# Softmax weights normalized ahead of their transposes instead of on the output

## The chip, the cores and the metric

The kernel runs on one core of a Trainium2 chip. Its time is the device time in microseconds of one execution, and lower is better. The engines of the core are TensorE (PE; its weight loads are listed as PEld), VectorE (DVE), ScalarE (ACT), GpSimd (POOL) and SyncE (SP), which here issues the DMAs. Each engine works through its own instructions in order; where an instruction waits, everything behind it on that engine waits too.

## The reference, cut to what matters

An attention over 8 batches, 12 heads, 448 positions and 64 elements per head feeds a gated feed-forward block.

```python
q_n, k_n = rmsnorm(q, g_q), rmsnorm(k, g_k)
scores = scale * np.matmul(q_n, k_n.transpose(0, 1, 3, 2))
scores = scores - np.max(scores, axis=-1, keepdims=True)
attn = np.exp(scores)
attn = attn / (np.sum(attn, axis=-1, keepdims=True) + 1e-09)
attn_out = np.matmul(attn, v)
...
h = gelu(x @ w_in)                       # x: attention output, heads side by side
u, v = h[..., :d_ff // 2], h[..., d_ff // 2:]
v_n = layernorm(v) * g_ln
v_s = np.einsum('ts,bsd->btd', w_sg, v_n) + b_sg[None, :, None]
out = x + (u * v_s) @ w_out
```

The division of the weights by their row sums is what the change moves. Since the sum belongs to a row of `attn`, the division can be made on the weights or, row by row, on the product with `v`.

## The kernel before, in words

Values are kept to more than 16 bits by splitting each into a high and a low f16 part and adding three products (high x high, high x low, low x high).

Heads are taken in pairs (48 pairs, `i`), and two pairs make a unit (24 units, `u`). The 448 rows of the two pairs of a unit are laid end to end, 896 rows, and cut into seven tiles of 128 rows (`t` = 0 to 6). Tile 3 holds the last 64 rows of the first pair and the first 64 of the second.

`scores(u)` (L375) goes through the seven tiles. For each, PE makes the scores of both heads, 128 rows by 2 x 448 (L389: 6 matmuls, 12 for tile 3), in a PSUM tile `s`, of which there are two (`NS`). DVE takes the negated maximum of each row and head (L392). ACT replaces the scores by their exponentials, one instruction per head, which also adds up the row (L394, with a short ACTIVATION_READ_ACCUMULATOR that writes the sum). After a `yield`, ACT copies the exponentials of both heads as f16 into `ahl` (L397), DVE subtracts that copy from the exponentials for the low part (L398), and SP issues the DMA transpose of the tile into `at_all` (L403). When L398 has ended, the PSUM tile is free for the next but one score tile.

`pv(i)` (L431) multiplies the transposed weights with `v` (L446, 24 matmuls) in the one buffer of the PSUM pool `ps_v` (`NV` = 1). The output has the 128 elements of the two heads on the partitions and the 448 positions along the free dimension. A row sum is therefore needed as a row along the free dimension, the same on all 64 partitions of a head. `recips(i)` (L406) makes it at the start of `pv`: POOL adds 1e-9 to the sums (L413), DVE takes reciprocals (L414), POOL splits them (L415, L416), PE multiplies each column, broadcast, with an identity matrix (L423, 16 matmuls per pair), and ACT copies the result to SBUF as `row` (L426). That product also uses the buffer of `ps_v`. At the end of `pv` DVE multiplies the output by `row` (L450), ACT copies it as f16 (L453) and DVE makes the low part (L454).

Around this run the preparation of q and k (`squares`, `norms`, `split`: L308 to L338), that of v (`vsquares`, `vscale`, `vsplit`: L343 to L371), the decoding of the weights at the start (`weights`) and, for each batch, the feed-forward block `moe` (L477).

The order of the work: all these are generators. The loop over pairs takes steps of `scores`, `pv`, `weights` and `moe` in turn, in the proportions of `SC`, `SV`, `WR` and `M0` to `ML`. The order in the program gives priorities, `moe` gets later ones by `MOFF`, and a planner (`schedule_with_timeline_sim`) then fixes each engine's order from its own estimate of durations. Semaphores are set from the data dependences. So a different set of instructions also gives a somewhat different order of the others.

Of the kernel before, what the change touches and what calls it, by code (L numbers as in the profile page):

```python
# [8 lines left out]
F32 = mybir.dt.float32  # L9
F32R = mybir.dt.float32r  # L10
F16 = mybir.dt.float16
BF16 = mybir.dt.bfloat16
I32 = mybir.dt.int32
AF = mybir.ActivationFunctionType
ALU = mybir.AluOpType
# [5 lines left out]
LEAST_SQ = (1.125 * 2.0 ** -15) ** 2  # L21
ASC = 2.0 ** 14


MOFF, MOFF0, GP = 200, 100, 350

# [5 lines left out]

VC, UC = (3,), (0, 1)

SC, SV = 7, 4

NS, NV, NM = 2, 1, 3
NQK, NVR, RAWB = 2, 2, 3
# [8 lines left out]
def kernel(  # L47
# [15 lines left out]
    B, H, S, D = q.shape  # L63
    P = 128
# [7 lines left out]
    HP = P // 2  # L72
    CM = S // P
    SM = CM * P
    CK = CM + 1
    C7 = 2 * CM + 1
    C4 = CM + 1
    NG = 2
# [4 lines left out]
    const = ctx.enter_context(tc.tile_pool(name="const", bufs=1))  # L83
    ld = ctx.enter_context(tc.tile_pool(name="ld", bufs=3))
    prep = ctx.enter_context(tc.tile_pool(name="prep", bufs=2))
    att = ctx.enter_context(tc.tile_pool(name="att", bufs=2))
    sml = ctx.enter_context(tc.tile_pool(name="sml", bufs=4))
    xp = ctx.enter_context(tc.tile_pool(name="xp", bufs=NX))
    ps_s = ctx.enter_context(tc.tile_pool(name="ps_s", bufs=NS, space=bass.MemoryType.PSUM))
    ps_v = ctx.enter_context(tc.tile_pool(name="ps_v", bufs=NV, space=bass.MemoryType.PSUM))  # L90
# [3 lines left out]
    V, A, G = nc.vector, nc.scalar, nc.gpsimd  # L94
    mm = nc.tensor.matmul
# [3 lines left out]
    G.memset(ones, 1.0)  # L99
    ident = const.tile([P, P], BF16, name="ident")  # L100
    make_identity(nc, ident)
    ident_h = const.tile([P, P], F16, name="ident_h")
    A.activation(out=ident_h, in_=ident, func=AF.Copy)
    swap = const.tile([P, P], F32, name="swap")
    for d, e in ((0, HP), (HP, 0)):
        V.tensor_copy(out=swap[:, d:d + HP], in_=ident[:, e:e + HP])
# [159 lines left out]
    R, U = {}, {}  # L266
    lo, hi = slice(0, HP), slice(HP, P)
# [107 lines left out]
    def scores(u):  # L375


        qt = U[u]["qt"]
        sums = sml.tile([P, C7, 2], F32, name="sums", bufs=2)
        U[u]["sums"] = sums  # L380
        for t in range(C7):
            ps = ps_s.tile([P, 2, 512], F32, name="s")

            rows = [(slice(0, P), t // C4)] if t != CM else [(lo, 0), (hi, 1)]
            for m, (qx, kx) in enumerate(((0, 2), (1, 2), (0, 3))):
                for h in range(2):
                    hs = slice(h * HP, (h + 1) * HP)
                    for r_, j in rows:
                        mm(out=ps[r_, h, 0:S], lhsT=qt[hs, qx, t * P + r_.start:t * P + r_.stop],  # L389
                           rhs=qt[hs, kx, j * S:(j + 1) * S], start=(m == 0), stop=(m == 2))  # L390
            nm = sml.tile([P, 2], F32, name="nm", bufs=6)
            V.tensor_reduce(out=nm, in_=ps[:, :, 0:S], axis=AX.X, op=ALU.max, negate=True)  # L392
            for h in range(2):
                A.activation(out=ps[:, h, 0:S], in_=ps[:, h, 0:S], func=AF.Exp, bias=nm[:, h:h + 1], accum_out=sums[:, t, h:h + 1])  # L394
            yield
            ahl = att.tile([P, 2, 2, S], F16, name="ahl", bufs=NAH)
            A.activation(out=ahl[:, 0], in_=ps[:, :, 0:S], func=AF.Copy)  # L397
            V.tensor_tensor(out=ahl[:, 1], in0=ps[:, :, 0:S], in1=ahl[:, 0], op=ALU.subtract)  # L398
            src = ahl.rearrange("p x h n -> p (x h n)")
            o = (NG * u * S + t * P) % (NAT * S)  # L400
            for r_ in ([slice(0, P)] if o + P <= NAT * S else [lo, hi]):
                o1 = (o + r_.start) % (NAT * S)
                nc.sync.dma_start_transpose(out=at_all[:, :, o1:o1 + r_.stop - r_.start], in_=src[r_])  # L403
            yield

    def recips(i):  # L406

        u, j = divmod(i, NG)
        cs = slice(0, C4) if j == 0 else slice(CM, C7)
        sums = U[u]["sums"][:, cs].rearrange("p t h -> p (t h)")  # L410
        x, y = (sml.tile([P, 2 * C4], F32, name=f"r{c}", bufs=2) for c in "xy")
        rh, rl = (sml.tile([P, 2 * C4], F16, name=f"r{c}", bufs=2) for c in "hl")
        G.tensor_scalar(out=x, in0=sums, scalar1=1e-9, scalar2=None, op0=ALU.add)  # L413
        V.reciprocal(out=y, in_=x)  # L414
        G.tensor_copy(out=rh, in_=y)  # L415
        G.tensor_tensor(out=rl, in0=y, in1=rh, op=ALU.subtract)  # L416
        ps = ps_v.tile([P, 512], F32, name="row", tag="pv")[:, 0:S]
        for n, t in enumerate(range(cs.start, cs.stop)):
            ks, o = (slice(0, P), t * P - j * S) if t != CM else ((lo, SM), (hi, 0))[j]
            for rx in (rh, rl):  # L420
                for h in range(2):
                    w = ks.stop - ks.start
                    mm(out=ps[h * HP:(h + 1) * HP, o:o + w], lhsT=rx[ks, 2 * n + h:2 * n + h + 1].broadcast_to([w, HP]),  # L423
                       rhs=ident_h[ks, ks], start=(n == 0 and rx is rh), stop=(n == CM and rx is rl), skip_group_check=True)
        row = att.tile([P, S], F32, name="row", bufs=1)
        A.activation(out=row, in_=ps, func=AF.Copy)  # L426
        return row

    XT = {}

    def pv(i):  # L431
        r = R[i]
        vh, vl = r["vh"], r["vl"]
        o = i % NAT * S

        steps = [[(slice(0, P), c + h * C4) if c < CM else (slice(h * HP, (h + 1) * HP), CM) for h in range(2)]
                 for c in range(C4)]
        blocks = [(vx, n, hx) for vx, n in ((vh, 0), (vl, 0), (vh, C7)) for hx in steps]

        blocks = blocks[CM::C4] + [x for n, x in enumerate(blocks) if n % C4 != CM]  # L440
        row = recips(i)
        yield
        ps = ps_v.tile([P, 512], F32, name="pv")[:, 0:S]
        for k_, (vx, n, hx) in enumerate(blocks):
            for h, (ks, c) in enumerate(hx):
                mm(out=ps[h * HP:(h + 1) * HP], lhsT=vx[ks, c], rhs=at_all[ks, n + c, o:o + S],  # L446
                   start=(k_ == 0), stop=(k_ == len(blocks) - 1), skip_group_check=True)
            if k_ in (4, 8):
                yield
        V.tensor_tensor(out=ps, in0=ps, in1=row, op=ALU.mult)  # L450
        xh = xp.tile([P, S], F16, name="xh")
        xl = xp.tile([P, S], F16, name="xl")
        A.activation(out=xh, in_=ps, func=AF.Copy)  # L453
        V.tensor_tensor(out=xl, in0=ps, in1=xh, op=ALU.subtract)  # L454
        XT[i] = (xh, xl)
        del R[i]

# [241 lines left out]
    for i in range(NI + 1):  # L699
        b, g = divmod(i, NP)  # L700
        u = i // NG
# [24 lines left out]
        if i < NI:  # L726
            if i % NG == 0:
                sc = scores(u)
            streams.append((sc, SC + 1 - 2 * (i % NG)))
        if i > 0:  # L730
            streams.append((pv(i - 1), SV))
# [16 lines left out]
        while True:  # L748
# [3 lines left out]
            x = min(todo, key=lambda x: (done[x] + 0.5) / streams[x][1])  # L752
# [39 lines left out]
```

## Time and profile before

| | |
|---|---|
| median of 3 runs | 1037.53 us |
| runs | 1032.77 to 1038.14 us |
| profiled execution | 1033.44 us |
| its span, first to last instruction | 1031.6 us |
| mean granted clock of TensorE in it | 0.916 |
| busy: PE, DVE, ACT, POOL | 829.0, 733.3, 738.1, 386.9 us |

A group's row gives its line, engine, operation, the tiles written and read, their shapes and its count; then its busy time in us and the mean of one in ns; then how long the engine had been idle just before instructions of the group, and what ended that. A row of the waits gives who waited for whom: us in total, times, and the longest. A row of the stretches gives the stretch and its length, then busy us (and instructions) of each engine, the share of TensorE's clock that was granted, the share of time in which DMA engines were busy, and GB/s. A row of the timeline gives start and duration in us. Lines such as L398 are those of the kernel before.

### The profile page before, as it was taken

What the parts mean: (1) busy time and instruction counts of PE and PEld (TensorE: products, weight loads), DVE (VectorE), ACT (ScalarE), POOL (GpSimd) and SP (SyncE); (2) the same over time, 40 slices, a digit from 0 to 9 for tenths busy, and PEclk for the clock granted to TensorE, in tenths of its full rate; (3) what the DMA queues carried; (4) which work ended last, traced back from release to release, by engine and by line L of the source; (5) the groups of instructions that cost most, each with busy time, mean ns of one, the idle gap of its engine ahead of it and who ended that gap; (6) DMA issues with size and microseconds to landing.
All of it is one profiled execution on the core that took longest, in us unless ns stands there. A gap on an engine that the chain in (4) does not pass through costs nothing.

```text
span 1031.6 us, 16639 instructions
## 1 busy us (share of the span) xinstructions
PE 829.0 (80%) x5844; PEld 421.1 (41%) x5844; DVE 733.3 (71%) x1332; ACT 738.1 (72%) x1449; POOL 386.9 (38%) x403
## 2 busy tenths in 40 slices
PE   0243666858798997899689998999779998998798
PEld 0111222324444563346234553446324563454246
DVE  6698888999587667786677758786669666766230
ACT  3767779877868767777768767987777776877351
POOL 1468614567253505243251606341533414030021
PEclk9976687969899999999699998999889999999899
DMA  6998748776886398478886488959967676556102
GB/s 163 214 228 191 166 115 196 185 176 130 181 197 150 88 204 180 98 170 145 186 175 147 99 194 183 182 123 176 194 142 160 141 166 125 106 135 123 40 1 62
DMA packets 448004, 155.70 MB, mean 151 GB/s; under 512 B 404336, under 2 KB 441776, under 8 KB 447920
## 3 DMA queue, kind: packets, MB, share of 16 engines
q1 hardware_dynamic: 447344, 154.18, 69.0%
q8 instruction: 46, 0.75, 0.3%
q10 hardware_dynamic: 576, 0.46, 0.2%
q14 instruction: 38, 0.31, 0.1%
HBM read 43.57 MB, written 11.01 MB: 53 GB/s over the span
## 4 chain that ended last, share of the span: by engine, by line
PE 34%; DVE 21%; ACT 19%; DMA 11%; issue 8%; SPq 4%; POOL 4%; ACTq 0%; POOLq 0%; DVEq 0%
PE pv L446 6%; ACT s L394 5%; DVE ahl L398 5%; PE s L389 4%; DVE nm L392 3%; ACT ahl L397 2%; DMA vr<-in_v_dram 2%; ACT sqk L308 2%; DMA raw<-in_moe_w_in_dram 2%; DMA at<-ahl 2%; POOL qk L330 2%; DMA qt<-hl 2%; DMA qk<-in_k_dram 2%; ACT hl L334 2%; SPq L336 1%
## 5 line engine op out<-in xcount | busy, mean ns | idle before, releaser
L394 ACT ACTIVATE s<-s,nm 128x448 f32<-128x448 f32 x336 | 204.0, 607 | 109.8 <-DVE nm L392 106.8
L398 DVE TENSOR_TENSOR ahl<-s,ahl 128x896 f16<-128x896 f32 x168 | 182.1, 1085 | 100.8 <-ACT ahl L397 99.8
L389 PE MATMUL s<-qt 64*128 64x448 f16 (+1 forms) x1152 | 143.2, 390 | 110.7 <-DVE ahl L398 76.4
L392 DVE TENSOR_REDUCE nm<-s 128x2 f32<-128x896 f32 x168 | 180.8, 1082 | 40.5 <-PE s L389 40.0
L397 ACT ACTIVATE ahl<-s 128x896 f16<-128x896 f32 x168 | 153.4, 920 | 5.3 <-DMA at<-ahl 3.1
L446 PE MATMUL pv<-at,vh 128*64 128x448 f16 (+1 forms) x768 | 122.7, 398 | 16.4 <-DMA at<-ahl 7.6
L413 POOL TENSOR_SCALAR rx<-sums 128x8 f32<-128x8 f32 x48 | 13.4, 278 | 311.8 <-ACT s L394 310.4
L389 PEld LDWEIGHTS <-qt 64*128 64x128 f16 (+1 forms) x1152 | 45.3, 102 | 177.2 <-issue 135.9
L330 POOL TENSOR_TENSOR qk<-qk,ny 128x896 f32<-128x896 f32 x46 | 80.8, 1774 | 85.8 <-DVE ny L125 82.3
L335 POOL TENSOR_TENSOR hl<-qk,hl 128x896 f16<-128x896 f32 x46 | 87.7, 1917 | 55.1 <-ACT hl L334 54.5
L568 PEld LDWEIGHTS <-wi 128*128 128x128 f16 x576 | 55.9, 100 | 60.2 <-issue 14.1
L446 PEld LDWEIGHTS <-vh 128*64 128x64 f16 (+1 forms) x768 | 43.4, 117 | 84.3 <-issue 70.2
L309 DVE TENSOR_REDUCE ss<-sqk 128x14 f32<-128x896 f32 x48 | 51.8, 1080 | 29.2 <-ACT sqk L308 28.9
L394 ACT ACTIVATION_READ_ACCUMULATOR s<-s,nm 128x1 f32 x336 | 67.7, 201 | 0.0
L329 POOL TENSOR_TENSOR qk<-qk,gg 128x896 f32<-128x896 f32 x23 | 48.0, 2085 | 43.2 <-ACT sqk L308 39.3
L423 PE MATMUL row<-ident_h,rh 128*64 128x128 f16 (+1 forms) x384 | 36.7, 240 | 31.7 <-POOL rh L415 24.0
L604 POOL TENSOR_TENSOR gt<-gt,u 128x448 f32<-128x448 f32 x32 | 38.5, 1206 | 60.1 <-DVE gt L603 55.9
L446 PE MATMUL pv<-at,vl 128*64 128x448 f16 (+1 forms) x384 | 60.4, 394 | 0.0
L334 ACT ACTIVATE hl<-qk 128x896 f16<-128x896 f32 x48 | 44.9, 947 | 15.9 <-POOL qk L330 8.4
L308 ACT ACTIVATE sqk<-qk 128x896 f32<-128x896 f32 x48 | 45.6, 951 | 8.2 <-DVE ss L309 4.4
L510 PEld LDWEIGHTS <-xh 128*128 128x128 f16 x288 | 27.0, 101 | 49.2 <-issue 21.9
L369 ACT ACTIVATE vh<-vr,v_s 128x448 f16<-128x448 f32 x48 | 31.9, 668 | 19.7 <-PE pv L446 19.6
(996 smaller groups left out, 1960.8 us busy)
## 6 DMA issues: line engine op xcount, KB each, us to landing
out_dram<-ot SPq DMA_DIRECT2D x56, 192.0 KB, 2.9
vr<-in_v_dram SPq DMA_DIRECT2D x32, 192.0 KB, 3.3
raw<-in_moe_w_in_dram SPq DMA_DIRECT2D x12, 512.0 KB, 5.7
qk<-in_q_dram SPq DMA_DIRECT2D x47, 128.0 KB, 2.8
qk<-in_k_dram SPq DMA_DIRECT2D x47, 128.0 KB, 2.8
vr<-in_v_dram SPq DMA_DIRECT2D x32, 144.0 KB, 3.3
qk<-in_q_dram SPq DMA_DIRECT2D x47, 96.0 KB, 2.6
qk<-in_k_dram SPq DMA_DIRECT2D x47, 96.0 KB, 2.6
```

The source lines that it names most:

```text
L308: A.activation(out=skv, in_=U[u]["qk"][:, x].rearrange("p h c d -> p (h c) d"), func=AF.Square)
L309: V.tensor_reduce(out=SS[u][:, x], in_=skv, axis=AX.X, op=ALU.add)
L330: E.tensor_tensor(out=qk, in0=qk, in1=r["rs"][:, x * SSW:(x + 1) * SSW].unsqueeze(2).broadcast_to([P, SSW, D]), op=ALU.mult)
L334: A.activation(out=h_, in_=r["qk"][:, x], func=AF.Copy)
L335: E.tensor_tensor(out=l_, in0=r["qk"][:, x], in1=h_, op=ALU.subtract)
L389: mm(out=ps[r_, h, 0:S], lhsT=qt[hs, qx, t * P + r_.start:t * P + r_.stop], rhs=qt[hs, kx, j * S:(j + 1) * S], start=(m == 0), stop=(m == 2))
L392: V.tensor_reduce(out=nm, in_=ps[:, :, 0:S], axis=AX.X, op=ALU.max, negate=True)
L394: A.activation(out=ps[:, h, 0:S], in_=ps[:, h, 0:S], func=AF.Exp, bias=nm[:, h:h + 1], accum_out=sums[:, t, h:h + 1])
L397: A.activation(out=ahl[:, 0], in_=ps[:, :, 0:S], func=AF.Copy)
L398: V.tensor_tensor(out=ahl[:, 1], in0=ps[:, :, 0:S], in1=ahl[:, 0], op=ALU.subtract)
L446: mm(out=ps[h * HP:(h + 1) * HP], lhsT=vx[ks, c], rhs=at_all[ks, n + c, o:o + S], start=(k_ == 0), stop=(k_ == len(blocks) - 1), skip_grou ...
L568: done = mm(out=ps[:, 0:S], lhsT=ww[:, g, f * P:(f + 1) * P], rhs=xx, start=(n == 0), stop=(n == 17))
```

## The change

Each tile's row sums get 1e-9 added and are divided by 2^10 on DVE, and DVE takes the reciprocals, two per row (one per head), right after the exponentials. The f16 copy is then made per head, scaled by that reciprocal, and the low part is made per head by a scalar_tensor_tensor that multiplies the exponentials by the reciprocal and subtracts the copy. The factor 2^10 is taken out again by a constant in the two instructions that end `pv`. `recips`, its identity matrix in f16 and the multiplication by `row` go. `pv` has one step less, and `SV` goes from 4 to 3.

```diff
+WSC = 2.0 ** 10
...
-SC, SV = 7, 4
+SC, SV = 7, 3
...
-    ident_h = const.tile([P, P], F16, name="ident_h")
-    A.activation(out=ident_h, in_=ident, func=AF.Copy)
...
-        sums = sml.tile([P, C7, 2], F32, name="sums", bufs=2)
-        U[u]["sums"] = sums
...
-            nm = sml.tile([P, 2], F32, name="nm", bufs=6)
+            nm, sums = (sml.tile([P, 2], F32, name=c, bufs=6) for c in ("nm", "sums"))
             V.tensor_reduce(out=nm, in_=ps[:, :, 0:S], axis=AX.X, op=ALU.max, negate=True)
             for h in range(2):
-                A.activation(out=ps[:, h, 0:S], in_=ps[:, h, 0:S], func=AF.Exp, bias=nm[:, h:h + 1], accum_out=sums[:, t, h:h + 1])
+                A.activation(out=ps[:, h, 0:S], in_=ps[:, h, 0:S], func=AF.Exp, bias=nm[:, h:h + 1], accum_out=sums[:, h:h + 1])
+            rc = sml.tile([P, 2], F32, name="rc", bufs=6)
+            V.tensor_scalar(out=sums, in0=sums, scalar1=1e-9, scalar2=1.0 / WSC, op0=ALU.add, op1=ALU.mult)
+            V.reciprocal(out=rc, in_=sums)
             yield
             ahl = att.tile([P, 2, 2, S], F16, name="ahl", bufs=NAH)
-            A.activation(out=ahl[:, 0], in_=ps[:, :, 0:S], func=AF.Copy)
-            V.tensor_tensor(out=ahl[:, 1], in0=ps[:, :, 0:S], in1=ahl[:, 0], op=ALU.subtract)
+            for h in range(2):
+                A.activation(out=ahl[:, 0, h], in_=ps[:, h, 0:S], func=AF.Copy, scale=rc[:, h:h + 1])
+                V.scalar_tensor_tensor(out=ahl[:, 1, h], in0=ps[:, h, 0:S], scalar=rc[:, h:h + 1], in1=ahl[:, 0, h],
+                                       op0=ALU.mult, op1=ALU.subtract)
...
-    def recips(i):
...
-        row = recips(i)
-        yield
         ps = ps_v.tile([P, 512], F32, name="pv")[:, 0:S]
...
-        V.tensor_tensor(out=ps, in0=ps, in1=row, op=ALU.mult)
...
-        A.activation(out=xh, in_=ps, func=AF.Copy)
-        V.tensor_tensor(out=xl, in0=ps, in1=xh, op=ALU.subtract)
+        A.activation(out=xh, in_=ps, func=AF.Copy, scale=1.0 / WSC)
+        V.scalar_tensor_tensor(out=xl, in0=ps, scalar=1.0 / WSC, in1=xh, op0=ALU.mult, op1=ALU.subtract)
```

More of the change, by code (lines that the diff above doesn't have):

```diff
@@ L404, in scores @@
             yield
-    def recips(i):
[L408 to L427, printed above, removed]
     XT = {}
```

## The prediction

> **What bounds the kernel now.** I read first the busy time of each engine, then the chain of work that ended last.
>
> ```profile
> PE 829.0 (80%) x5844; PEld 421.1 (41%) x5844; DVE 733.3 (71%) x1332; ACT 738.1 (72%) x1449; POOL 386.9 (38%) x403
> ...
> PE 34%; DVE 21%; ACT 19%; DMA 11%; issue 8%; SPq 4%; POOL 4%; ACTq 0%; POOLq 0%; DVEq 0%
> ```
>
> No engine is full and the chain runs through three of them. TensorE (PE) is the fullest, VectorE (DVE) and ScalarE (ACT) stand close behind. Next come the busy times by stretch (columns: PE, PEld, DVE, ACT, POOL, granted clock, DMA share, GB/s).
>
> ```profile
> 50.00:225.00 175.00, 98.70 (x624) 41.30 (x624) 158.85 (x280) 134.86 (x266) 96.71 (x79) 0.73 0.80 181
> 225.00:925.00 700.00, 630.22 (x4572) 325.71 (x4570) 509.15 (x931) 532.25 (x1055) 263.46 (x285) 0.95 0.72 154
> ```
>
> There are two regimes. From 50 to 225 us DVE is busy 158.85 / 175 = 91% and bounds (it also prepares the weights). From 225 to 925 us PE is busy 90%, DVE 73%, ACT 76%: there PE comes nearest to a bound. Last, who waits for whom, and how one score tile is handed on:
>
> ```profile
> PE s L389 <- DVE ahl L398: 76.4, 35, 9.0
> PE row L423 <- POOL rh L415: 24.0, 13, 5.3
> ...
> L398 DVE TENSOR_TENSOR ahl<-s,ahl x168: 1027/1091/1093, 30.8 to 961.7; 128x896 f16<-128x896 f32 x168
> ```
>
> ```profile
> 504.68 0.91 ACT L397 ACTIVATE ahl<-s 128x896 f16<-128x896 f32 x1
> ...
> 505.63 1.09 DVE L398 TENSOR_TENSOR ahl<-s,ahl 128x896 f16<-128x896 f32 x1 [0.89 <-ACT ahl L397]
> ...
> 506.78 1.30 PE L389 MATMUL s<-qt 64*128 64x448 f16 x6 [0.39 <-DVE ahl L398]
> ```
>
> PE's largest wait is for the subtraction of L398, since that ends the use of a score tile in PSUM, and there are only two such tiles. A handoff takes 0.04 us (505.59 to 505.63) to 0.06 us. The 168 tiles follow each other every (961.7 - 30.8) / 167 = 5.57 us, so a tile may occupy its place for 11.1 us before PE must wait for it.
>
> **What the change removes.** The rows of reciprocals go from PE, POOL, DVE and ACT, and so does the multiplication of the output on DVE.
>
> ```profile
> 0.00:1031.60 1031.60, 41.38 (x768) 28.36 (x768) 0.92 0.70 151
> ```
>
> This is PE and PEld at L423 alone (its busy time counted once where matmuls overlap): 41.4 us of PE. The wait for POOL above it, 24.0 us, goes as well.
>
> ```profile
> L413 POOL TENSOR_SCALAR rx<-sums 128x8 f32<-128x8 f32 x48 | 13.4, 278 | 311.8 <-ACT s L394 310.4
> L414 DVE RECIPROCAL ry<-rx 128x8 f32<-128x8 f32 x48 | 9.4, 196 | 15.8 <-POOL rx L413 15.5
> L415 POOL CAST rh<-ry 128x8 f16<-128x8 f32 x48 | 9.6, 201 | 28.7 <-DVE ry L414 22.6 <-DVE ly L122 1.4 <-DVE xt L618 1.4
> L416 POOL TENSOR_TENSOR rl<-ry,rh 128x8 f16<-128x8 f32 x48 | 10.5, 218 | 3.6
> L426 ACT ACTIVATE row<-row 128x448 f32<-128x448 f32 x48 | 26.0, 542 | 6.5 <-PE row L423 6.3
> L450 DVE TENSOR_TENSOR pv<-pv,row 128x448 f32<-128x448 f32 x48 | 30.0, 624 | 22.3 <-PE pv L446 22.0 <-PE mo__6671 L636 0.4
> ```
>
> POOL loses 33.5 us, DVE 9.4 + 30.0 = 39.4 us, ACT 26.0 us. POOL's 310.4 us of waiting at L413 stand at the head of an in-order queue, but POOL is busy only 38% and has 4% of the chain; I count the removed busy time there and nothing for the wait.
>
> **What it adds.** These rows carry the prices:
>
> ```profile
> L398 DVE TENSOR_TENSOR ahl<-s,ahl 128x896 f16<-128x896 f32 x168 | 182.1, 1085 | 100.8 <-ACT ahl L397 99.8 <-issue 0.3
> L603 DVE SCALAR_TENSOR_TENSOR gt<-ms__6148,gw,bb 128x448 f32<-128x448 f32 x1 | 0.7, 676 | 0.0
> L454 DVE TENSOR_TENSOR xl<-pv,xh 128x448 f16<-128x448 f32 x48 | 29.5, 614 | 2.8 <-ACT xh L453 2.8
> L370 DVE SCALAR_TENSOR_TENSOR vl<-vr,v_s,vh 128x448 f16<-128x448 f32 x48 | 36.6, 764 | 3.0 <-ACT vh L369 3.0
> L538 DVE TENSOR_SCALAR mv<-mv 128x2 f32<-128x2 f32 x6 | 1.0, 169 | 0.2
> L397 ACT ACTIVATE ahl<-s 128x896 f16<-128x896 f32 x168 | 153.4, 920 | 5.3 <-DMA at<-ahl 3.1
> L394 ACT ACTIVATE s<-s,nm 128x448 f32<-128x448 f32 x336 | 204.0, 607 | 109.8 <-DVE nm L392 106.8
> L453 ACT ACTIVATE xh<-pv 128x448 f16<-128x448 f32 x48 | 25.9, 540 | 18.4 <-DVE pv L450 18.4
> L369 ACT ACTIVATE vh<-vr,v_s 128x448 f16<-128x448 f32 x48 | 31.9, 668 | 19.7 <-PE pv L446 19.6
> ```
>
> (The row of L538 is that of the stretch 225 to 925 us.) DVE, per tile: the one subtraction of 1.085 becomes two scalar_tensor_tensor of 128x448 from PSUM with a per-partition scalar. L603 is the same operation with the same sources but an f32 output: 0.676 each. The two small operations cost 0.169 (L538) and 0.196 (L414, with 8 elements instead of 2). So 2 x 0.676 + 0.365 - 1.085 = +0.63 us, times 168 = +106 us. L454 becomes the three-operand form, 48 x 0.06 = +3. Less 39.4: DVE +70 us net. Bounds: with 0.614 each and 0.300 for the pair, +35; with 0.764 and 0.4, +110. The first fits only if the scalar costs nothing, the second reads SBUF; L603 is nearest.
>
> ACT: one copy of 0.920 becomes two with a scale per partition. The nearest row is L394, which also reads PSUM and takes a per-partition operand, 0.607: 336 x 0.607 - 153.4 = +51, less 26.0 = +25 us. Bounds from L453 and L369: +2 and +45. Accumulating the sums is there before as after.
>
> The score stream's DMA transposes keep their number, size and queue. The second copy lies beside the first subtraction, so from the start of the copy to the release of the tile it is 0.607 + 2 x 0.676 = 1.96 us against 0.920 + 1.085 = 2.0 us before; I count nothing there. Without that cover (ACT busy elsewhere between the two copies) it is the 0.607 us of the second copy more. One tile of constants less at the start is nothing. SV 4 to 3 follows the one step that pv loses; it shifts the planned order by an amount that I cannot price, from -5 to +5 us; I take 0.
>
> **The new wait.** Before, the copy of L397 follows the exponentials on ACT itself. After, ACT's copy waits for DVE's reciprocal, which waits for ACT's sums. Behind the two small operations on DVE stand the next tile's maximum (L392) and other tiles' subtractions, and behind ACT's copy the next exponentials. I count two handoffs (0.1 us), half an operation of L398's size already running on DVE at 78% busy (0.42) and some 0.2 for ACT to come back: 0.7 us more for each tile in its PSUM place, beside 0.365 already counted. PE waited for such a place 35 times: 35 x 0.7 = +25 us. Lower bound 0 (other work fills it), upper bound all tiles with two places, 168 x 0.7 / 2 = +59.
>
> **The sum.** Busy time is worth what the chain holds of it: PE 0.34 x 1031.6 / 829.0 = 0.42 per busy us, DVE 0.21 x 1031.6 / 733.3 = 0.30, ACT 0.19 x 1031.6 / 738.1 = 0.27, POOL 0.04 x 1031.6 / 386.9 = 0.11. For PE I take 0.6, between 0.42 and its 0.90 share in the long stretch.
>
> PE -41.4 x 0.6 = -25. DVE +70 x 0.30 = +21. ACT +25 x 0.27 = +7. POOL -33.5 x 0.11 = -4. PE's wait for the rows, -24, of which half comes back: the same place in PE's order next waits for the transposes of the last tile, which land later than its sums: -12. The new wait +25. In the early stretch DVE weighs 0.91 and not 0.30:
>
> ```profile
> 50.00:225.00 175.00, 28.13 (x26) 0.73 0.80 181
> ...
> 50.00:225.00 175.00, 4.35 (x7) 0.73 0.80 181
> ```
>
> L398 runs there 26 times and L450 7 times, 26 x 0.63 - 7 x 0.82 = +10.6 us, so another 10.6 x 0.61 = +6. Together +18 us: 1033.4 (the profiled execution: a span of 1031.6 and 1.8 around it) becomes 1051. That execution lies 4 us below the median of 1037.5, inside the runs' 1032.8 to 1038.1, and I leave 1051 as the forecast.
>
> **A rule of the skill against the PE term.** PE's clock follows its work: 0.73 at 56% busy and 0.95 at 90% in the stretches above. At (630 - 30) / 715 = 84% the line between them gives about 0.91, and 600 us of PE work would take 4% or 26 us more, which is the whole -25. The Trainium skill, "TensorE: Matmul & The Clock Gate", Part 1, says that the clock halves after an idle window of about 3.4 us; by that rule only long gaps matter, not the mean share, and the -25 would stand. The trace's stretches cannot tell the two apart.
>
> **Rivals.**
> (a) PE is the bound, and its relief comes through: -41.4 x 0.90 = -37, the whole wait of -24, POOL -4, against DVE +21, ACT +7, the early stretch +6 and a third of the new wait, +8, for the tiles that find no other matmul to run: 1033.4 - 23 = 1010. For it: PE's 90% in the long stretch. Against: DVE at (509 + 70 x 0.68) / 677 = 82% and ACT at (532 + 25 x 0.68) / 677 = 81% (0.68 is the stretch's share of the span) would then have to run fuller than now. It decides if PE's waits for L398 stay near 76 us.
> (b) It cancels: the terms are as in the sum, but only a third of the new wait shows, since PE's order has other matmuls to run meanwhile: +18 - 17 = +1, 1034, and 1033 to 1042 with the unpriced order. For it: 133 of 168 tiles do not keep PE waiting now. Against: 99.8 us of DVE's idle time and 106.8 us of ACT's (rows of L398 and L394) are already waits of one for the other at score tiles.
> (c) DVE becomes the bound: its +70 at 0.91 and no gain on PE: 1033.4 + 64 = 1097. The Trainium skill, "Perfetto Trace Analysis", Identifying the Most-Contended Engine, calls matmul busy time a poor measure and wants weight loads instead. By that rule PEld's 41% makes ACT's 72% and DVE's 71% the bounds, and this rival's price holds. Against it: PE's 34% of the chain.
>
> **Chances.** Forecast (1042 to 1072) 0.43, (a) 0.30, (b) 0.18, (c) 0.09. Differences under 0.5% (5 us) cannot be told from none here. Forecast and (c) give slower 0.52; (a) faster 0.30, (b) the same 0.18. Range: from the middle of (a), rounded, to about half-way between forecast and (c), 1011 to 1076; the likeliest case alone spans 1042 to 1072.
>
> **What would show it.** Each step: DVE busy near 803 us and ACT near 763; the new subtraction near 0.676, the copy near 0.607; no L423 on PE; PE's wait for the last subtraction above 76 us, a new wait of ACT's copy for the reciprocal, and DVE's for the sums. If PE's waits at score tiles do not grow, or the long stretch gets shorter, the step of the new wait is wrong; if the granted clock falls with PE's share, the line through the two stretches was right.

## The result

The changed kernel takes 1172.95 us (median of 4 runs, 1171.8 to 1174.0) where the kernel before takes 1036.4 beside it: a ratio of 1.132, with a 95% interval from 1.129 to 1.136. It is slower by 136.5 us. The forecast was 1051 with a range up to 1076.

The profile's busy times and the long stretch of the changed kernel (columns as for the kernel before):

```profile
PE 815.9 (70%) x5076; PEld 407.0 (35%) x5076; DVE 807.1 (69%) x1740; ACT 773.4 (66%) x1568; POOL 348.7 (30%) x259
```

```profile
225.00:925.00 700.00, 536.20 (x3387) 270.40 (x3384) 500.84 (x1088) 481.95 (x985) 211.85 (x154) 0.87 0.61 136
```

Every engine has a smaller share of the span than before, DVE and ACT too, though both got more work. So no engine took over as the bound; all of them wait more. PE's share of the long stretch falls from 90% to 77%, and its granted clock from 0.95 to 0.87. (The chain of waits of this profile breaks off after a few per cent of the span and is not used.)

The groups of the score tiles, which answer to L398, L394, L397, L392, L413, L414 and L453 of before, in this order:

```profile
L400 DVE SCALAR_TENSOR_TENSOR ahl<-s,rc,ahl 128x448 f16<-128x448 f32 x336 | 225.6, 679 | 107.8 <-ACT ahl L399 106.7
L392 ACT ACTIVATE s<-s,nm 128x448 f32<-128x448 f32 x336 | 203.5, 606 | 141.5 <-DVE nm L390 138.0
L399 ACT ACTIVATE ahl<-s,rc 128x448 f16<-128x448 f32 x336 | 208.8, 632 | 106.0 <-DVE ahl L400 55.9 <-ACT s L392 20.0 <-issue 19.0
L390 DVE TENSOR_REDUCE nm<-s 128x2 f32<-128x896 f32 x168 | 180.8, 1081 | 15.6 <-PE s L387 15.6
L394 DVE TENSOR_SCALAR sums<-sums 128x2 f32<-128x2 f32 x168 | 49.7, 296 | 88.6 <-ACT s L392 87.9
L395 DVE RECIPROCAL rc<-sums 128x2 f32<-128x2 f32 x168 | 27.4, 163 | 4.1
L430 ACT ACTIVATE xh<-pv 128x448 f16<-128x448 f32 x48 | 25.9, 539 | 18.8 <-PE pv L424 18.6
```

Two waits are new. DVE stands idle 87.9 us for ACT's sums, as foreseen. And ACT's copy (L399) waits 55.9 us for DVE's subtraction (L400), which was not foreseen: a copy of one head has no data in common with the subtraction of the other. The other wait that was foreseen, ACT's copy standing idle for the reciprocal (L395), comes to 4.1 us only (6 times). What all this leads to is in PE's waits:

```profile
PE s L387 <- DVE ahl L400: 173.9, 69, 11.6
...
PE pv L424 <- DMA at<-ahl: 40.4, 19, 7.6
```

PE's wait for a free score tile has gone from 76.4 us (35 times) to 173.9 us (69 times), and its wait for the transposes from 7.6 us (row of L446 below, under no_norm) to 40.4. One tile in the timeline, first ACT, then DVE, then PE:

```profile
798.32 0.63 ACT L399 ACTIVATE ahl<-s,rc 128x448 f16<-128x448 f32 x1 [0.48 <-ACT s L392]
...
799.70 0.63 ACT L399 ACTIVATE ahl<-s,rc 128x448 f16<-128x448 f32 x1 [0.37 <-DVE ahl L400]
```

```profile
797.86 0.17 DVE L394 TENSOR_SCALAR sums<-sums 128x2 f32<-128x2 f32 x1 [2.46 <-ACT s L392]
798.07 0.17 DVE L395 RECIPROCAL rc<-sums 128x2 f32<-128x2 f32 x1
798.98 0.68 DVE L400 SCALAR_TENSOR_TENSOR ahl<-s,rc,ahl 128x448 f16<-128x448 f32 x1 [0.75 <-ACT ahl L399]
799.58 1.08 DVE L390 TENSOR_REDUCE nm<-s 128x2 f32<-128x896 f32 x1
800.58 0.68 DVE L400 SCALAR_TENSOR_TENSOR ahl<-s,rc,ahl 128x448 f16<-128x448 f32 x1
```

```profile
801.31 0.74 PE L387 MATMUL s<-qt 64*128 64x448 f16 x6 [0.28 <-DVE ahl L400]
```

The first copy ends at 798.95, the first subtraction runs from 798.98 to 799.66, and only then, at 799.70, does the second copy start. While DVE waits for it, it takes up the maximum of another tile (L390, until 800.66), and the second subtraction comes after that. From the start of the first copy to the release it is 2.94 us, where the prediction had 1.96. (Over all 168 tiles, worked out from the traces, this part takes 4.02 us in the mean, and 2.53 in the kernel before.) The two halves alternate strictly: in all 168 tiles the second copy starts only after the first subtraction has ended, although the two share no data and only read different halves of the same PSUM tile. Where they read an SBUF tile instead (exp_sbuf, below), every second copy starts before the first subtraction has ended.

### The profile page after: what moved, and what is told of

Its sections match the earlier page's. It is cut to its first block, busy times and chain, and to the rows that moved or that the text cites. A ratio compares the mean times of both kernels' runs of the same rounds, so it can differ in the third digit from the quotient of the medians.

```text
span 1172.2 us, 15382 instructions
## 1 busy us (share of the span) xinstructions
PE 815.9 (70%) x5076; PEld 407.0 (35%) x5076; DVE 807.1 (69%) x1740; ACT 773.4 (66%) x1568; POOL 348.7 (30%) x259
## 5 line engine op out<-in xcount | busy, mean ns | idle before, releaser
L400 DVE SCALAR_TENSOR_TENSOR ahl<-s,rc,ahl 128x448 f16<-128x448 f32 x336 | 225.6, 679 | 107.8 <-ACT ahl L399 106.7
L392 ACT ACTIVATE s<-s,nm 128x448 f32<-128x448 f32 x336 | 203.5, 606 | 141.5 <-DVE nm L390 138.0
L387 PE MATMUL s<-qt 64*128 64x448 f16 (+1 forms) x1152 | 150.3, 405 | 206.4 <-DVE ahl L400 173.9
L399 ACT ACTIVATE ahl<-s,rc 128x448 f16<-128x448 f32 x336 | 208.8, 632 | 106.0 <-DVE ahl L400 55.9
L390 DVE TENSOR_REDUCE nm<-s 128x2 f32<-128x896 f32 x168 | 180.8, 1081 | 15.6 <-PE s L387 15.6
L424 PE MATMUL pv<-at,vh 128*64 128x448 f16 (+1 forms) x768 | 130.7, 432 | 50.0 <-DMA at<-ahl 40.4
L387 PEld LDWEIGHTS <-qt 64*128 64x128 f16 (+1 forms) x1152 | 49.3, 104 | 290.8 <-issue 219.8
L394 DVE TENSOR_SCALAR sums<-sums 128x2 f32<-128x2 f32 x168 | 49.7, 296 | 88.6 <-ACT s L392 87.9
L424 PEld LDWEIGHTS <-vh 128*64 128x64 f16 (+1 forms) x768 | 46.8, 126 | 124.0 <-issue 98.8
L424 PE MATMUL pv<-at,vl 128*64 128x448 f16 (+1 forms) x384 | 67.7, 437 | 0.0
L392 ACT ACTIVATION_READ_ACCUMULATOR s<-s,nm 128x1 f32 x336 | 66.3, 197 | 0.0
L431 DVE SCALAR_TENSOR_TENSOR xl<-pv,xh 128x448 f16<-128x448 f32 x48 | 29.6, 617 | 22.4 <-ACT xh L430 22.2
L370 DVE SCALAR_TENSOR_TENSOR vl<-vr,v_s,vh 128x448 f16<-128x448 f32 x48 | 40.5, 844 | 0.0
```

Source lines behind the costliest of these rows:

```text
L394: V.tensor_scalar(out=sums, in0=sums, scalar1=1e-9, scalar2=1.0 / WSC, op0=ALU.add, op1=ALU.mult)
L399: A.activation(out=ahl[:, 0, h], in_=ps[:, h, 0:S], func=AF.Copy, scale=rc[:, h:h + 1])
L400: V.scalar_tensor_tensor(out=ahl[:, 1, h], in0=ps[:, h, 0:S], scalar=rc[:, h:h + 1], in1=ahl[:, 0, h], op0=ALU.mult, op1=ALU.subtract)
```

## The experiments

To compare runs, the table below gives two times worked out from the start and end of each instruction in the trace, over all 168 score tiles: how long a tile is held in PSUM (from its first matmul to the end of the last instruction that uses it there; mean), and the interval from one tile's first matmul to the next one's (mean). With two tiles in PSUM, twice the interval is the held time plus the time a place stands empty. Both times are those of the profiled execution, which is 6.8 us faster than the median in copies_first, and 5.5 and 7.9 us slower in busy_only and exp_sbuf_rows.

The planner also gives each kernel its own order, so no two of these kernels differ in the edit alone. Counted in the traces, PE has run the same number of matmuls before a score tile starts in only 65 of the 168 tiles for the changed kernel and copies_first, and in 87 for the changed kernel and sv4. The last pair differs in the order alone, and by 21 us. A step of a few tens of us in this table may therefore be order in part.

| kernel | median us | held us | interval us |
|---|---|---|---|
| before | 1036 | 9.62 | 5.60 |
| no_norm | 1030.7 | 9.79 | 5.56 |
| forms_only | 1046.7 | 9.93 | 5.67 |
| busy_only | 1077.9 | 10.21 | 5.88 |
| whole_rc | 1110.1 | 10.50 | 6.03 |
| split_only | 1125.0 | 10.42 | 6.14 |
| copies_first | 1134.0 | 10.69 | 6.14 |
| changed kernel | 1173.0 | 11.49 | 6.43 |
| sv4 | 1193.8 | 11.42 | 6.54 |
| held | 1171.9 | 11.50 | 6.42 |
| exp_sbuf | 1017.6 | 8.99 | 5.47 |
| exp_sbuf_rows | 1012.8 | 8.02 | 5.37 |
| exp_sbuf_pool | 991.0 | 8.49 | 5.26 |
| no_norm_sbuf | 973.4 | 7.58 | 5.06 |

### Both copies first (copies_first)

```diff
             for h in range(2):
                 A.activation(out=ahl[:, 0, h], in_=ps[:, h, 0:S], func=AF.Copy, scale=rc[:, h:h + 1])
+            for h in range(2):
                 V.scalar_tensor_tensor(out=ahl[:, 1, h], in0=ps[:, h, 0:S], scalar=rc[:, h:h + 1], in1=ahl[:, 0, h],
                                        op0=ALU.mult, op1=ALU.subtract)
```

> The changed kernel, with both halves' copies ahead of both halves' subtractions; all else and all results the same. In the changed kernel the second copy starts 35 ns after the first subtraction ends in most tiles, so the halves alternate: copy, subtraction, copy, subtraction, each a handoff between ACT and DVE. Theory 1 (the alternation is the loss): with one handoff instead of three a score tile stays 11.3 - 1.0 = about 10.3 us in PSUM, 1.0 x 168 / 2 = 84 us less, so about 1090 us. Rival 2 (the round trip exponentials - reciprocal - copy is the loss): 1150 to 1175 us, since that wait stays. Rival 3 (the added busy time of DVE and ACT): 1165 to 1175 us, since it stays too.

Measured: 1133.97 us, ratio to before 1.095 [1.090, 1.099]. So 39 us of the 136.5 go when the alternation goes, with the same instructions, and rivals 2 and 3 did not foresee that. But Theory 1's 1090 is missed: the tile is held 0.8 us less and not 1.0, and 98 us of loss remain.

### The cut alone (split_only)

```diff
-            A.activation(out=ahl[:, 0], in_=ps[:, :, 0:S], func=AF.Copy)
-            V.tensor_tensor(out=ahl[:, 1], in0=ps[:, :, 0:S], in1=ahl[:, 0], op=ALU.subtract)
+            for h in range(2):
+                A.activation(out=ahl[:, 0, h], in_=ps[:, h, 0:S], func=AF.Copy)
+                V.tensor_tensor(out=ahl[:, 1, h], in0=ps[:, h, 0:S], in1=ahl[:, 0, h], op=ALU.subtract)
```

> The kernel before, with its copy and its subtraction cut into one of each per head, alternating; the rows of reciprocals and the multiplication of the output stay. Theory 1: most of the loss shows here, about 1036 + 100 = 1136 us, with DVE's and ACT's waits for each other at the halves. Rival 2: only the added busy time, 168 x (2 x 0.614 - 1.085) = 24 us on DVE and 27 us on ACT at a third of their value, 1036 to 1060 us. Rival 3: the same 1036 to 1060 us, as half of the added busy time is here.

Measured: 1124.99 us, ratio 1.085 [1.082, 1.089]: 89 us for cutting two instructions into four, without any normalization ahead. PE's waits in it:

```profile
PE s L389 <- DVE ahl L399: 66.0, 37, 6.6
PE row L424 <- POOL rh L416: 55.2, 18, 10.9
```

Here PE's wait for score tiles does not grow by itself (76.4 before); its wait for the rows of reciprocals does, from 24.0 to 55.2 us. The sums that the rows need come from the same tiles, which now come later, and the rows' matmuls stand in PE's order; that this is why is argued only. The loss was near what Theory 1 said; the place where it shows was not. The two waits together grow by 20.8 us, so they hold only a part of the 89, and where the rest arises stays open.

### The relief alone (no_norm)

```diff
-            rc = sml.tile([P, 2], F32, name="rc", bufs=6)
-            V.tensor_scalar(out=sums, in0=sums, scalar1=1e-9, scalar2=1.0 / WSC, op0=ALU.add, op1=ALU.mult)
-            V.reciprocal(out=rc, in_=sums)
...
-            for h in range(2):
...
+            A.activation(out=ahl[:, 0], in_=ps[:, :, 0:S], func=AF.Copy)
+            V.tensor_tensor(out=ahl[:, 1], in0=ps[:, :, 0:S], in1=ahl[:, 0], op=ALU.subtract)
```

> The relief alone: the changed kernel without any normalization (no reciprocals at all; whole-tile copy and subtraction as in the kernel before). It leaves out the division by the row sums. Theory 1 and both rivals: the removal is worth 15 to 45 us, so 990 to 1020 us; if it is 1030 us or more, the rows of reciprocals cost nothing before and my term for PE was empty.

Measured: 1030.67 us, ratio 0.995 [0.993, 0.997]. Taking the rows of reciprocals and the multiplication away, and putting nothing in their place, gains 5 us. The stated alternative holds, by less than 1 us: what the removal frees is not on the path that sets the time. PE's first two waits, and below them the second one's row in the kernel before, say where it went:

```profile
PE s L387 <- DVE ahl L396: 119.1, 53, 10.1
PE pv L419 <- DMA at<-ahl: 30.8, 10, 6.1
```

```profile
PE pv L446 <- DMA at<-ahl: 7.6, 3, 3.0
```

PE no longer waits 24.0 us for the rows, and waits 42.7 us more for score tiles and 23.2 us more for the transposes.

### The round trip without the cut (whole_rc)

```diff
-            for h in range(2):
-                A.activation(out=ahl[:, 0, h], in_=ps[:, h, 0:S], func=AF.Copy, scale=rc[:, h:h + 1])
...
+            A.activation(out=ahl[:, 0], in_=ps[:, :, 0:S], func=AF.Copy, scale=rc[:, 0:1])
+            V.scalar_tensor_tensor(out=ahl[:, 1], in0=ps[:, :, 0:S], scalar=rc[:, 0:1], in1=ahl[:, 0], op0=ALU.mult, op1=ALU.subtract)
```

> The changed kernel with the round trip but without the cut: the reciprocals are made as in it, and one copy and one scalar_tensor_tensor of the whole tile take the first head's reciprocal for both heads (the second head's own reciprocal is left out). Theory 1: beside the run without normalization only the round trip is added, 0.5 to 0.9 us per tile in PSUM, so 25 to 70 us more than that run and about 1050 us. Rival 2: nearly all of the loss is here, 1140 to 1170 us. Rival 3: DVE has 168 x (1.717 - 1.45) = 45 us less than in the changed kernel, 1130 to 1150 us.

Measured: 1110.05 us, ratio 1.072 [1.069, 1.075]; 79 us above the run without normalization. All three missed: the round trip costs more than Theory 1 allowed, it is not "nearly all" (rival 2), and the time is 20 us below rival 3's range. From here to the kernel with both copies first are 24 us (the cut without the alternation), and 39 more to the changed kernel.

### What the round trip consists of (forms_only, busy_only)

The first takes `sums[:, 0:1]` as the scale, without the two small operations; the second keeps them and takes a constant:

```diff
-            A.activation(out=ahl[:, 0], in_=ps[:, :, 0:S], func=AF.Copy, scale=rc[:, 0:1])
+            A.activation(out=ahl[:, 0], in_=ps[:, :, 0:S], func=AF.Copy, scale=sums[:, 0:1])
```

```diff
-            A.activation(out=ahl[:, 0], in_=ps[:, :, 0:S], func=AF.Copy, scale=rc[:, 0:1])
+            A.activation(out=ahl[:, 0], in_=ps[:, :, 0:S], func=AF.Copy, scale=cst)
```

The subtraction takes the same scale in each.

> The run without normalization, but copy and subtraction of the whole tile take the first head's row sum as a per-partition scale (in place of the reciprocals, which are left out): the operand forms of the changed kernel without DVE's two small operations and without a wait for DVE. If the longer forms are what the whole-tile round trip lost (79 us), 1100 us or more. If the wait for DVE is (theory 1), within 10 us of the run without normalization, 1025 to 1045 us.

> The whole-tile run with the round trip, but copy and subtraction take their scale from a constant; DVE still makes the reciprocals and nothing uses them (the normalization is left out). If DVE's 168 pairs of small operations, 77 us busy in the changed kernel, and their waits for ACT's sums in DVE's order are what is lost, 1090 to 1110 us. If it is ACT's wait for the reciprocal before the copy, 1035 to 1060 us.

Measured: 1046.74 us (ratio 1.008 [1.006, 1.011]) and 1077.92 us (1.038 [1.032, 1.043]). So 1030.7 to 1046.7 is the longer operand forms (16 us), to 1077.9 the small operations in DVE's order (31 us), to 1110.1 the copy's dependence on them (32 us). The last is a step between two times and not a wait that the profile shows: ACT's copy stands idle for the reciprocal for 7.9 us in whole_rc (6 times), while from the end of the exponentials to the start of the copy a tile takes 2.03 us in the mean there and 0.91 in busy_only. The steps are rough, too, since the four runs of busy_only lie between 1069.1 and 1083.4 us. Forms_only lies just above the range of the wait's theory and far from the other. Neither expectation of busy_only fits: it lies between the two.

### The exponentials in SBUF (exp_sbuf)

```diff
+            ex = att.tile([P, 2, S], F32, name="ex", bufs=2)
...
-                A.activation(out=ps[:, h, 0:S], in_=ps[:, h, 0:S], func=AF.Exp, bias=nm[:, h:h + 1], accum_out=sums[:, h:h + 1])
+                A.activation(out=ex[:, h], in_=ps[:, h, 0:S], func=AF.Exp, bias=nm[:, h:h + 1], accum_out=sums[:, h:h + 1])
...
-                A.activation(out=ahl[:, 0, h], in_=ps[:, h, 0:S], func=AF.Copy, scale=rc[:, h:h + 1])
-                V.scalar_tensor_tensor(out=ahl[:, 1, h], in0=ps[:, h, 0:S], scalar=rc[:, h:h + 1], in1=ahl[:, 0, h],
+                A.activation(out=ahl[:, 0, h], in_=ex[:, h], func=AF.Copy, scale=rc[:, h:h + 1])
+                V.scalar_tensor_tensor(out=ahl[:, 1, h], in0=ex[:, h], scalar=rc[:, h:h + 1], in1=ahl[:, 0, h],
```

> The changed kernel with the exponentials written to an SBUF tile (two of them) in place of PSUM; results are the same. The score tile in PSUM is then free after the exponentials, about 6 us after its start instead of 11.3, and ACT's second copy no longer has to wait for DVE's first subtraction. Reading SBUF costs DVE about 168 x 2 x 0.1 = 34 us of busy time more. Theory 1 (time in PSUM, made long by the alternation and the round trip, is the loss): 1030 to 1075 us. Rival 2 and 3 (round trip and busy time in the engines' own orders, whatever the place of the tile): 1120 to 1180 us.

Measured: 1017.60 us, ratio 0.980 [0.978, 0.983]. The change's whole loss is gone and the kernel is 155 us faster than the changed one, more than Theory 1 foresaw, with more work on DVE:

```profile
PE 789.4 (78%) x5076; PEld 396.2 (39%) x5076; DVE 855.5 (84%) x1740; ACT 754.9 (74%) x1568; POOL 384.2 (38%) x259
...
L401 DVE SCALAR_TENSOR_TENSOR ahl<-ex,rc,ahl 128x448 f16<-128x448 f32 x336 | 297.7, 916 | 12.4 <-ACT ahl L400 12.2
...
L400 ACT ACTIVATE ahl<-ex,rc 128x448 f16<-128x448 f32 x336 | 202.9, 663 | 25.8 <-issue 7.0
```

ACT's copy no longer waits for DVE's subtraction, and DVE's wait for the copy falls from 106.7 to 12.2 us. PE still waits for score tiles, now for the exponentials that free them, and longer than the 76.4 us in the kernel before, so this wait alone does not measure the loss:

```profile
PE s L387 <- ACT ex L393: 103.6, 43, 9.7
```

### Held in PSUM again (held)

The edit of exp_sbuf frees the PSUM tile early and also lifts the alternation. To part the two, one element of the score tile is read after the second subtraction:

```diff
+            keep = sml.tile([P, 1], F32, name="keep", bufs=6)
+            V.scalar_tensor_tensor(out=keep, in0=ps[:, 1, S - 1:S], scalar=rc[:, 1:2], in1=ahl[:, 1, 1, S - 1:S], op0=ALU.mult, op1=ALU.add)
```

> The run with the change and the exponentials in SBUF (1017.6 us), but a one-element DVE operation that reads the score tile after the second subtraction keeps the tile in PSUM as long as the changed kernel does; its result is used nowhere. ACT's second copy still need not wait for DVE's first subtraction. If the time in PSUM is what is lost (theory 1a), 1100 to 1150 us. If the forced alternation of the halves on ACT and DVE is (theory 1b), 1015 to 1045 us: the added operations are 168 x 0.17 = 29 us of DVE at most.

Measured: 1171.89 us, ratio 1.129 [1.128, 1.131]. That is the changed kernel's time, to 1 us, with the same held time (11.50 and 11.49 us), and PE's waits again:

```profile
PE s L387 <- DVE keep L404: 194.1, 64, 11.1
```

The added operations are 35.9 us of DVE:

```profile
L404 DVE SCALAR_TENSOR_TENSOR keep<-s,rc,ahl 128x1 f32<-128x1 f32 x168 | 35.9, 214 | 2.4
```

154 us cannot come from these 35.9. The time lies 22 us above the range of theory 1a and 127 us above that of theory 1b. So the loss comes with the time for which a score tile keeps its place in PSUM, as theory 1a has it: here every second copy starts before the first subtraction has ended, and the loss is there all the same. The alternation is one of the things that make the held time long, and this run shows no cost of it beside that. That the held times agree to 0.01 us is chance: from the copy's start to the end of the second subtraction a tile takes 3.07 us here and 4.02 in the changed kernel, but the added read comes 0.72 us later, and the copy starts 2.05 us after the exponentials and not 1.63.

One thing the run does not part from the held time is the planned order. With a place free early the planner puts score tiles earlier among PE's work: by 99 matmuls in the mean from held to exp_sbuf, with the same number in only 7 of the 168 tiles. How much of the 154 us is PE's wait at run time and how much this order was not tested.

### The same edit in the kernel before (exp_sbuf_rows)

The edit is that of exp_sbuf, with the whole-tile copy and subtraction of before and `NX` 12 to 11.

> The kernel before with the exponentials written to an SBUF tile (two of them; one buffer less for the pairs' outputs, 11 for 12, to make room). Results are the same. Theory 1: the kernel before waits for score tiles too (76.4 us of PE's idle time), so it gains up to that less the longer reads of SBUF: 990 to 1025 us. Rivals 2 and 3: 1040 to 1070 us, since the reads get longer and nothing is won.

Measured: 1012.79 us, ratio 0.976 [0.973, 0.979]. The kernel before was held up by the same two places. With the place in PSUM free early, the change costs 4.8 us (1017.6 against 1012.8) and not 136.5. Those 4.8 us cannot be told from none: one of the five runs here took 1020.7, and this kernel has 11 buffers for the pairs' outputs against 12 in exp_sbuf.

### What the removal is worth then (no_norm_sbuf)

The edit of exp_sbuf in the kernel of no_norm.

> The run without any normalization (the division by the row sums is left out), with the exponentials in SBUF: the relief from the rows of reciprocals where the score tiles in PSUM no longer hold PE up, against 1012.8 us with the rows. If PE was the next bound, as my rival (a) had it, 960 to 985 us. If the rows' work lay in gaps, 1000 to 1012 us.

Measured: 973.38 us, ratio 0.938 [0.936, 0.940]. The rows are worth 39 us here (1012.8 to 973.4), against 5 us where score tiles are held in PSUM until the subtraction. (This kernel has 12 buffers for the pairs' outputs, exp_sbuf_rows 11; what that difference is worth was not measured.)

### The step of the stream (sv4)

```diff
-SC, SV = 7, 3
+SC, SV = 7, 4
```

> The changed kernel with SV = 4 as before in place of 3: only the proportion in which the output's steps are traced among the others, and so the planned order, differs. All theories: within 12 us of the changed kernel, 1160 to 1185 us; if it is 1120 us or less, a good part of the loss was the order that went with SV = 3.

Measured: 1193.77 us, ratio 1.150 [1.148, 1.152]. All theories missed: the planned order alone is worth 21 us here, and `SV` = 3 is the better one, so it did not cause the loss.

### A faster kernel (exp_sbuf_pool)

```diff
-            V.tensor_scalar(out=sums, in0=sums, scalar1=1e-9, scalar2=1.0 / WSC, op0=ALU.add, op1=ALU.mult)
+            G.tensor_scalar(out=sums, in0=sums, scalar1=1e-9, scalar2=1.0 / WSC, op0=ALU.add, op1=ALU.mult)
```

> The run with the change and the exponentials in SBUF, with the addition of 1e-9 moved from DVE to POOL; results are the same. DVE is 84% busy in that run and loses 168 x 0.17 to 0.30 = 29 to 50 us; two handoffs are added, but no score tile in PSUM waits for them. If DVE's work is now the bound, 985 to 1005 us; if the handoffs count or POOL's order holds the sums back, 1018 us or more.

Measured: 990.96 us, ratio 0.955 [0.954, 0.957], the fastest of the kernels that leave nothing out, 4.5% below the kernel before.

```profile
PE 777.7 (79%) x5076; PEld 396.9 (40%) x5076; DVE 781.3 (79%) x1572; ACT 752.8 (76%) x1568; POOL 426.6 (43%) x427
```

DVE has 74 us less than in exp_sbuf, where 29 to 50 were expected: the addition took 0.358 us in the mean there and not 0.17 to 0.30. That the added handoffs cost less than this now, where the copy's dependence on the reciprocals cost 32 us in whole_rc, fits the held time: they no longer lie in it.

## Why the prediction was wrong, point by point

**The prices of the instructions held.** DVE was put at 803 us and has 807.1; the new subtraction at 0.676 and takes 0.679; ACT at 763 and has 773.4. The copy was put at 0.607 by the exponential's row and takes 0.632, against 0.539 for the same copy with a constant scale (L430). The Trainium skill, "ScalarE: Activation LUTs", What ACT_TABLE_LOAD costs, gives about 93 ns for each per-partition operand, and 0.632 - 0.539 agrees. The small addition takes 0.296 and not 0.169 on average, though its median is the 0.169 that was predicted:

```profile
L394 DVE TENSOR_SCALAR sums<-sums x168: 151/169/1882, 28.2 to 1100.8; 128x2 f32<-128x2 f32 x168
```

Worked out from the trace, the 127 additions that overlap no instruction of POOL take 0.167 us in the mean, and the 41 that do take 0.696. None of this is the error: exp_sbuf has 48 us more on DVE than the changed kernel and is 155 us faster.

**The first step that failed: "I count nothing there".** The second copy was to lie beside the first subtraction. It starts after it. I named the cost without that cover as 0.607 us, but as a case in which ACT is busy elsewhere, and left it out of the sum. It holds in every tile: from the start of the copy to the release a tile takes 4.02 us in the mean and not 2.53 as before, where I had 1.96 and 2.0. With both copies first it is 2.77, and 39 us less (copies_first against the changed kernel).

**The second step that failed: the new wait, +25.** The 0.7 us that I put on a tile were about right for the round trip itself: it lengthens the held time by 0.71 us (no_norm to whole_rc), and from the end of the exponentials to the start of the copy a tile takes 1.63 us in the mean and not 0.85 as before. What was mis-sized is for how many tiles it counts: I priced it at the 35 tiles for which PE waited, with half of all tiles as the far bound, and the round trip cost 79 us where that far bound was 59. In all, the tile is held 1.87 us longer (9.62 to 11.49), the round trip's 0.71 and the alternation's 0.80 (copies_first to the changed kernel) being the largest parts. In the kernel before, a place stands empty 2 x 5.60 - 9.62 = 1.58 us between two tiles; I took that for slack which could swallow most of the new wait. In the changed kernel it is 2 x 6.43 - 11.49 = 1.37 us, so it shrank by 0.21 us only. That (1.87 - 0.21) x 168 / 2 = 139 us comes near the 136.5 measured is no test, since interval, held time and empty time are tied to each other by definition; it says that the empty time swallowed little. Nor has a held microsecond one price: the round trip's 0.71 us cost 79 us, the alternation's 0.80 only 39, and sv4 holds its tiles 0.07 us less than the changed kernel and takes 21 us more. What keeps a place empty for so long was not tested; that PE has other matmuls ahead in its order is argued only.

**The third: PE's relief, -25, and half of the wait for the rows, -12.** The removal alone gained 5 us. The share that PE had of the chain did not say that less work on PE shortens it: PE's freed time became waits for score tiles (76.4 to 119.1 us) and for the transposes (7.6 to 30.8 us): of the 24.0 us for the rows, nearly all came back there and not half. The relief is real, 39 us, once tiles leave PSUM early.

**The order, "from -5 to +5 us".** It is worth 21 us between `SV` = 3 and 4. My bound had no row behind it.

**The clock.** The line through the two stretches gives 0.73 + 0.22 x (77 - 56) / 34 = 0.87 at 77% busy, and 0.87 was granted. PE is busy 815.9 us and not 829.0 - 41.4 = 788, so about 28 us of its relief in busy time are gone; a matmul of the scores takes 405 ns in the mean and not 390. Whether the lower clock also lengthens the time is not shown, since PE waits meanwhile. Waits of up to 11.6 us stand in the changed kernel, so the rule of "TensorE: Matmul & The Clock Gate" (the Trainium skill), Part 1, by which only long gaps count, fits as well, and which of the two holds stays open.

**The rivals.** (c), DVE as the bound, came nearest in time (1097) and is wrong in cause: its busy share fell to 69%. (a) was right about PE only where score tiles leave PSUM early. None of the three named the place in PSUM as the limit, though the prediction had 5.57 us for each tile and two places, so 11.1 us, and only missed to ask how much of the 11.1 a tile uses (9.62).

## What to carry to other kernels

Where a stage works on a tile in a place of which there are few, add up how long the place is held, from the first write to the last read, and divide by the number of places: where that is near the interval between tiles (here 4.81 of 5.60 us), time added to the holding can count for all tiles, whatever the engines' busy shares. Before cutting an instruction into two on a shared PSUM tile, see in a trace whether the halves on two engines will overlap at all; if they only take turns, the cut adds handoffs to the held time. Copying out early (here: the exponentials written to SBUF by the instruction that makes them anyway) can be worth more than the work that one removes from the engines: 24 us in the kernel before, against 5 us for the rows of reciprocals.

## What the runs showed of the hardware

DVE's subtraction with both sources in SBUF takes as long as from PSUM if GpSimd is idle (0.676 and 0.680 us) and much longer if it is not (1.25). The instruction rows (min/median/max) of the changed kernel and of exp_sbuf:

```profile
L400 DVE SCALAR_TENSOR_TENSOR ahl<-s,rc,ahl x336: 658/683/686, 31.7 to 1103.3; 128x448 f16<-128x448 f32 x168
```

```profile
L401 DVE SCALAR_TENSOR_TENSOR ahl<-ex,rc,ahl x336: 654/678/2430, 35.3 to 944.2; 128x448 f16<-128x448 f32 x168
```

The medians are the same, 0.683 and 0.678 us, but from SBUF single ones take up to 2.43 us. A stretch of exp_sbuf's timeline, DVE and then POOL:

```profile
599.73 1.28 DVE L401 SCALAR_TENSOR_TENSOR ahl<-ex,rc,ahl 128x448 f16<-128x448 f32 x2
...
601.93 2.27 DVE L401 SCALAR_TENSOR_TENSOR ahl<-ex,rc,ahl 128x448 f16<-128x448 f32 x2
```

```profile
601.91 1.14 POOL L585 TENSOR_TENSOR gl<-gt,gh 128x448 fp32r<-128x448 f32 x1 [2.41 <-ACT gh L583]
```

The same two subtractions take 1.28 us at 599.73 and 2.27 us at 601.93, just after an instruction of POOL started that lasts until 603.05. Over all 336 of them, worked out from the trace, the 195 that overlap no elementwise instruction of POOL take 0.676 us in the mean, and the 141 that do take 1.25 us. In the changed kernel, which reads the exponentials from PSUM, the 102 that overlap take 0.677 us and the other 234 take 0.680. The Trainium skill, "SBUF — State Buffer", Who interferes with whom, says that a DVE instruction with two SBUF inputs contends with a GpSimd instruction that reads SBUF, and that the order of issue decides which of the two blocks. The trace agrees: of the 141, the 109 that started after the POOL instruction take 1.39 us in the mean, and the 32 that started before it 0.75. The move to SBUF cost DVE 72 us this way (297.7 against 225.6), and paid all the same.
